# Attention and two MLPs on one Trainium2 core: sums of x on VectorE, parts of x and slices of w_out prepared over several steps, prepared weights' loads begun at the end of MLP 1

## The chip, the cores and the metric

The program runs on one NeuronCore of a Trainium2 chip. TensorE (PE) does the matrix products, VectorE (DVE), ScalarE (ACT) and GpSimd (POOL) the rest, and SyncE (SP) issues the DMAs. Every engine executes its own instructions in order and waits on semaphores for the others. The metric is the device time of one execution in microseconds (us).

## The reference

A chunked attention with eight memory keys (4 batches, 8 heads, 768 positions of 64) gives x, 3072 tokens by 512. Two MLPs follow one another, each with a hidden width of 2048:

```
h = x @ w1_in;  y = (h - tanh(h)) @ w1_out
h = y @ w2_in;  g = h if h >= 1, 0 if h <= -1, else (h + 1)^2 / 4
out = g @ w2_out
```

The weights come as 64-bit floats, all else is 32-bit. The four weight matrices of the two MLPs are rounded to 32 bits on the chip.

## The kernel before

**Precision.** Each operand of a weight product is split into a high part (rounded, by ACT: `split_to`, L203) and the rest (the low part, by VectorE, L204). A product is hi·hi + lo·hi + hi·lo. A 64-bit weight slice is rounded by two ACT passes (`round_act`, L131 and L134), three VectorE operations (L140, L141, L149) and one integer add (L153), here on GpSimd.

**MLP 1.** Tokens are cut into 6 blocks of 512, the hidden width into 16 slices of 128: 96 steps. Step s computes one hidden slice (`hidden`, 12 matmuls of 512 columns) and the output slice of step s-16 (`second`, 12 matmuls). Attention runs between the steps until about step 78. When MLP 1's steps end, 17 of its output slices are left ("old").

**Preparing MLP 2's weights.** In steps 32 to 81 the slices of w2_in are rounded, summed (`prep_sums`), split and stored to DRAM (`win`, seven tiles for each of 8 pairs). The 16 slices of w2_out go the same way to `wout` (`prep_out_*`), eight beside the w_in pairs and eight in steps 88 to 95 (`PREP_OUT`).

**MLP 2.** The first product works on pairs of token blocks (3 superblocks, `sb`) and pairs of hidden slices (8, `q`) by a scheme with seven products in place of eight on 2x2 blocks. One pair is a quad (`quad`, n = 0 to 23): the products run in the order 1, 2, 6, 5, 7, 4, 3, each 6 matmuls on a part of x (`xc`) and streamed tiles of `win` (`in`). Products 1, 6, 7, 4 accumulate in bank a; ACT copies the bank out in between as u1, u2, u3. Products 2, 5 and 3 use banks b and c, of which there is one pair. `gate2` makes the four hidden slices of a quad: an add with u1, u2 or u3 and a clamp on VectorE, a square on ACT, a maximum on VectorE. After products 2, 5, 7 and 3 stands a gap (`gap`, 0 to 3): an output slice of 12 matmuls, first the 17 old ones, then those of MLP 2, whose `ghi` (ACT) and `glo` (VectorE) are prepared one gap ahead and whose weights stream in from `wout` (`out`).

**What sets the order.** Code order is each engine's order; buffers are reused by tag, and an instruction waits until its buffer is free. Up to MLP 2 three tables of events (`before`, `rounds`, `behind`) put work at steps. SP's DMAs form one queue: x for a superblock (`x_load`, four of 512 KB), `in` (256 KB), `out` (256 KB), slices to be rounded (`stage`, 512 KB) and stores. Between superblocks x's seven parts are made in the last quad of the old superblock, each right behind the product that used the old part; the sums of x run on GpSimd (`x_sums`, L544 to L548).

Of the kernel before, what the change touches and what calls it, by code (L numbers as in the profile page):

```python
# [57 lines left out]
PREP_OUT = [37 + 7 * i for i in range(8)] + [88 + i for i in range(8)]  # L58
# [4 lines left out]
STREAM_IN, STREAM_OUT = 10, 8  # L63

# [9 lines left out]
def tile_memory_attention_two_mlps(  # L74
# [71 lines left out]
    def round_sign(phase, which, fc):  # L146
# [6 lines left out]
        nc.gpsimd.tensor_tensor(out=bits, in0=bits, in1=stage[:, :, 0], op=ALU.add)  # L153
# [38 lines left out]
    def prep_sums(q):  # L192
# [5 lines left out]
        for o, a, b in ((t1, b12, b11), (t3, b22, b12), (t2, b22, t1), (t4, b21, t2)):  # L198
            nc.gpsimd.tensor_tensor(out=o, in0=a, in1=b, op=ALU.subtract)
# [25 lines left out]
    def prep_out_load(fc):  # L225
        load_weights(1, 1, fc, "stage3" if fc < HALF else f"stage{fc % STAGES}")
# [306 lines left out]
    def x_sums(sb, part):  # L533
        f = held[sb]
        if part == 0:
            f["tags"] = []
            for i in (5, 6):
                two = [take(f"a{i}_{sb}_{k}") for k in range(2)]
                f["tags"] += [tag for tag, _ in two]
                f[i] = [t for _, t in two]  # L540
# [15 lines left out]
    def x_split(sb, i):  # L556
        if i in XWIDE:
# [7 lines left out]
        for k in range(2):  # L565
            split_to(f[:, k, :] if i not in (5, 6) else f[k], t[k], t[2 + k])
        if i == 2:
            x_sums(sb, 1)
        if i in (5, 6):
            for tag in held[sb]["tags"][2 * (i - 5):2 * (i - 4)]:  # L570
                give_later.append(tag) if i == 6 else give(tag)
        if i == 3:
            for tag in give_later:
# [86 lines left out]
    def ready(item, n, gap):  # L660
# [4 lines left out]
        return need < n - 1 or (need == n - 1 and gap >= 2)  # L665
# [143 lines left out]
    for fc in range(FC):  # L809
        p = PREP_OUT[fc]  # L810
# [11 lines left out]
    def x_give(fc):  # L822
# [156 lines left out]
```

## Time and profile before

| | us |
|---|---|
| median of 3 runs | 1178.83 |
| lowest and highest | 1177.38, 1179.82 |
| the profiled execution | 1177.54 |
| its span, first to last instruction | 1175.8 |
| PE busy | 1111.2 |
| VectorE busy | 759.8 |
| ACT busy | 556.9 |
| GpSimd busy | 155.4 |

The span is cut in 40 slices, each with the busy share in tenths. A row of the timeline says when a run of like instructions starts, how long it lasts, and in square brackets how long the engine was idle before it and who ended that. "x6" is a count; start times are us from the span's start. MLP 2 begins at about 600 us. A DMA's issue on SP is not its landing; where landing is given, it is from issue.

### The profile page before, as it was taken

To read this page: it belongs to the slowest core of one execution; us is meant where nothing else is said; L and a number is where in the kernel's file an instruction comes from. 1 tells how busy PE (TensorE), PEld (TensorE's weight loads), DVE (VectorE), ACT (ScalarE), POOL (GpSimd) and SP (SyncE) were. 2 spreads that over 40 slices of the span, in tenths; PEclk is the share of its full clock that TensorE was granted. 3 is DMA by queue.
4 is the path that set the end of the run, shared out by engine and by line. 5 is a ranking of instruction groups with operands and counts; after the bars stand their busy time and mean duration, and the time that the engine had idled before them with its cause. 6 is when DMAs were issued, how large, how long until landed. Compare 5 with 4: busy or idle time off the path is not lost.

```text
span 1175.8 us, 20216 instructions
## 1 busy us (share of the span) xinstructions
PE 1111.2 (95%) x7793; PEld 899.2 (76%) x7799; DVE 759.8 (65%) x1252; ACT 556.9 (47%) x964; POOL 155.4 (13%) x126
## 2 busy tenths in 40 slices
PE   6999999999999999999659999789999989999998
PEld 3677888888888888888448878668887868888876
DVE  4799987887887788679846554644454644353532
ACT  3566665566555566556534433423233433333321
POOL 1231220221222022025200020100020100000000
PEclk9999999999999999999969999989999999999999
DMA  9895643634644641453253465436576546556264
GB/s 232 238 264 173 165 135 99 181 113 157 198 153 127 195 155 46 153 188 126 108 196 109 151 218 195 160 115 234 188 251 224 187 148 226 183 198 233 101 227 146
DMA packets 159648, 202.67 MB, mean 172 GB/s; under 512 B 61760, under 2 KB 86336, under 8 KB 159552
## 3 DMA queue, kind: packets, MB, share of 16 engines
q1 hardware_dynamic: 159552, 201.38, 53.9%
q8 instruction: 62, 1.02, 0.4%
q14 instruction: 34, 0.28, 0.1%
HBM read 165.68 MB, written 35.65 MB: 171 GB/s over the span
## 4 chain that ended last, share of the span: by engine, by line
PE 84%; DVE 7%; ACT 4%; DMA 2%; issue 1%; SPq 1%; POOL 0%; DVEq 0%; ACTq 0%; POOLq 0%
PE h L461 21%; PE acc L496 21%; PE acc_n L496 21%; PE qa L617 10%; PE qb L617 7%; DVE xc L204 2%; PE a L365 1%; PE a L309 1%; DVE g L651 1%; ACT xc L203 1%; PE b L351 1%; DVE wlo L172 1%; DVE glo L204 1%; DMA in<-win 1%; DVE g L644 1%
## 5 line engine op out<-in xcount | busy, mean ns | idle before, releaser
L204 DVE TENSOR_TENSOR glo<-g,ghi 128x512 fp32r<-128x512 f32 x192 | 141.7, 739 | 162.2 <-ACT ghi L203 111.8
L496 PE MATMUL acc_n<-ghi,out 128*128 128x512 f32 x768 | 199.4, 398 | 18.6 <-ACT ghi L203 14.0
L496 PEld LDWEIGHTS acc_n<-ghi,out 128*128 128x128 f32 x768 | 145.6, 191 | 54.7 <-ACT ghi L203 16.0
L617 PE MATMUL qa<-xc,in 128*128 128x512 f32 x576 | 148.2, 393 | 20.2 <-DMA in<-win 20.2
L203 ACT ACTIVATE ghi<-g 128x512 fp32r<-128x512 f32 x192 | 119.5, 625 | 82.9 <-PE acc L496 48.5
L172 DVE TENSOR_TENSOR wlo<-raw,whi 128x512 fp32r<-128x512 f32 x192 | 147.9, 770 | 4.7 <-ACT whi L165 4.7
L648 ACT ACTIVATE t<-t,half 128x512 f32<-128x512 f32 x96 | 69.5, 724 | 165.2 <-DVE t L647 164.9
L153 POOL TENSOR_TENSOR raw<-raw,stage 128x512 int32<-128x512 int32 x64 | 84.2, 1316 | 461.3 <-DVE raw L149 319.0
L617 PEld LDWEIGHTS qa<-xc,in 128*128 128x128 f32 x576 | 109.1, 190 | 44.2 <-issue 20.6
L165 ACT ACTIVATE whi<-raw 128x512 fp32r<-128x512 f32 x192 | 120.5, 628 | 24.4 <-PE acc L496 17.2
L644 DVE TENSOR_TENSOR g<-qb,u 128x512 f32<-128x512 f32 x72 | 49.7, 690 | 121.9 <-ACT u L633 90.6
L633 ACT ACTIVATE u<-qa 128x512 f32<-128x512 f32 x72 | 42.9, 596 | 147.7 <-PE qa L617 147.5
L617 PE MATMUL qb<-xc,in 128*128 128x512 f32 x432 | 111.1, 393 | 1.1 <-DVE g L644 1.1
L496 PE MATMUL acc<-ghi,whi 128*128 128x512 f32 x384 | 109.6, 399 | 0.2 <-ACT y L506 0.2
L461 PE MATMUL h<-xh,whi 128*128 128x512 f32 (+2 forms) x392 | 105.7, 391 | 3.0 <-ACT whi L165 3.0
L496 PE MATMUL acc_n<-glo,out 128*128 128x512 f32 x384 | 107.0, 393 | 0.0
L496 PE MATMUL acc<-ghi,wlo 128*128 128x512 f32 x384 | 106.0, 390 | 0.2 <-DVE wlo L172 0.2
L496 PE MATMUL acc<-glo,whi 128*128 128x512 f32 x384 | 105.6, 389 | 0.0
L471 ACT ACTIVATE g<-h 128x512 f32<-128x512 f32 x96 | 57.0, 594 | 102.3 <-PE h L461 80.6
L461 PE MATMUL h<-xh,wlo 128*128 128x512 f32 (+2 forms) x392 | 104.1, 387 | 1.0 <-DVE wlo L172 1.0
L461 PE MATMUL h<-xl,whi 128*128 128x512 f32 (+2 forms) x392 | 103.8, 387 | 0.1
L617 PEld LDWEIGHTS qb<-xc,in 128*128 128x128 f32 x432 | 81.8, 190 | 19.1 <-DVE g L644 2.0
(88 smaller groups left out, 1390.0 us busy)
## 6 DMA issues: line engine op xcount, KB each, us to landing
out<-wout SPq DMA_DIRECT2D x192, 256.0 KB, 2.9
in<-win SPq DMA_DIRECT2D x168, 256.0 KB, 3.5
stage<-w_in SPq DMA_DIRECT2D x32, 512.0 KB, 5.4
stage<-w_out SPq DMA_DIRECT2D x32, 512.0 KB, 4.0
k<-qkv_t SPq DMA_DIRECT2D x80, 128.0 KB, 4.5
v<-qkv_t SPq DMA_DIRECT2D x80, 128.0 KB, 3.3
win<-preph SPq DMA_DIRECT2D x32, 256.0 KB, 3.3
yd<-y SPq DMA_DIRECT2D x24, 256.0 KB, 2.6
```

What stands on the lines that cost most here:

```text
L153: nc.gpsimd.tensor_tensor(out=bits, in0=bits, in1=stage[:, :, 0], op=ALU.add)
L165: nc.scalar.activation(out=hi, in_=r, func=AF.Copy)
L172: nc.vector.tensor_tensor(out=lo, in0=r, in1=hi.bitcast(F32), op=ALU.subtract)
L203: nc.scalar.activation(out=hi, in_=src, func=AF.Copy)
L204: nc.vector.tensor_tensor(out=lo, in0=src, in1=hi.bitcast(F32), op=ALU.subtract)
L461: nc.tensor.matmul(hp, w[:, kc * 128:(kc + 1) * 128], x[:, kc, n0:n1], start=j == 0 and kc == 0, stop=j == 2 and kc == KC - 1,)
L471: nc.scalar.activation(out=g, in_=hp, func=AF.Tanh)
L496: nc.tensor.matmul(acc_t[dm], w[:, dm * 128:(dm + 1) * 128], g, start=first and j == 0, stop=last and j == 2,)
L617: nc.tensor.matmul(bank, w[:, k * 128:(k + 1) * 128], z[k], start=first and j == 0 and k == 0, stop=j == 2 and k == 1, skip_group_check=True,)
L633: nc.scalar.activation(out=t, in_=bank, func=AF.Copy)
L644: nc.vector.tensor_tensor(out=g, in0=src, in1=plus, op=ALU.add)
L648: nc.scalar.activation(out=t, in_=t, func=AF.Square, scale=0.5, bias=half)
```

## The change

In MLP 1 the integer add of the second MLP's rounding and the sums of w_in and of x go from GpSimd to VectorE. x's first superblock is loaded at step 80 and cut in steps 82 to 91, except parts 4 and 3, which are cut in quad 0. Only eight slices of w_out are prepared in MLP 1; the others, two a quad, in quads 0 to 3 (`late_out`). The first seven `in` loads are written into steps 93 and 94. At later superblocks the sums come in quads 4, 5 and 7, parts 1 and 2 are cut in quad 6 into tiles of their own where needed (`xnext`), the others after gaps of quad 7 and of the next quad. The 17 old output slices take four gaps in quads 0 and 1 and three in quads 2 to 4 (`OLD_GAPS`), an MLP 2 slice may be used one gap earlier, and the prefetch of `out` begins in quad 3 instead of 2, `x_load` in the quad 3 of a superblock instead of its quad 4.

```diff
...
 PREP_IN, PREP_IN_EVERY = 32, 7
-PREP_OUT = [37 + 7 * i for i in range(8)] + [88 + i for i in range(8)]
+OLD_GAPS = [(0, 1, 2, 3)] * 2 + [(0, 1, 2)] * 3
...
-        nc.gpsimd.tensor_tensor(out=bits, in0=bits, in1=stage[:, :, 0], op=ALU.add)
+        eng = nc.vector if phase else nc.gpsimd
+        eng.tensor_tensor(out=bits, in0=bits, in1=stage[:, :, 0], op=ALU.add)
...
         for o, a, b in ((t1, b12, b11), (t3, b22, b12), (t2, b22, t1), (t4, b21, t2)):
-            nc.gpsimd.tensor_tensor(out=o, in0=a, in1=b, op=ALU.subtract)
+            nc.vector.tensor_tensor(out=o, in0=a, in1=b, op=ALU.subtract)
         sums_t[q] = t
...
     def prep_out_load(fc):
-        load_weights(1, 1, fc, "stage3" if fc < HALF else f"stage{fc % STAGES}")
+        load_weights(1, 1, fc, "stage3")
...
-    def x_sums(sb, part):
+    def x_sums(sb, k):
         f = held[sb]
...
+        for i in (5, 6):
+            f[i] = f.get(i, []) + [take(f"a{i}_{sb}_{k}")]
+        a11, a12, a21, a22 = (f[i][:, k, :] for i in (1, 2, 7, 4))
+        s1, s2 = f[5][k][1], f[6][k][1]
+        nc.vector.tensor_tensor(out=s1, in0=a21, in1=a22, op=ALU.add)
+        nc.vector.tensor_tensor(out=s2, in0=s1, in1=a11, op=ALU.subtract)
+        nc.vector.tensor_tensor(out=a21, in0=a11, in1=a21, op=ALU.subtract)
+    def x_sum_last(sb):
+        f = held[sb]
         for k in range(2):
-            a11, a12, a21, a22 = (f[i][:, k, :] for i in (1, 2, 7, 4))
-            if part == 0:
-                nc.gpsimd.tensor_tensor(out=f[5][k], in0=a21, in1=a22, op=ALU.add)
-                nc.gpsimd.tensor_tensor(out=f[6][k], in0=f[5][k], in1=a11, op=ALU.subtract)
-                nc.gpsimd.tensor_tensor(out=a21, in0=a11, in1=a21, op=ALU.subtract)
-            else:
-                nc.gpsimd.tensor_tensor(out=a12, in0=a12, in1=f[6][k], op=ALU.subtract)
-        if part == 1:
-            f[3] = f[2]
-    xc = {}
+            a12 = f[2][:, k, :]
+            nc.vector.tensor_tensor(out=a12, in0=a12, in1=f[6][k][1], op=ALU.subtract)
+        f[3] = f[2]
+    xc, xnext = {}, {}
...
     def x_split(sb, i):
-        if i in XWIDE:
+        if i in (1, 2) and sb % 2:
+            two = [
+                wide.tile([128, 2, N], F32R, tag=f"stage{2 * i - 2 + k}", name=f"xc{i}_{sb}_{k}") for k in range(2)
+            ]
+            t = [two[k // 2][:, k % 2, :] for k in range(4)]
+        elif i in XWIDE:
             t = xsp.tile([128, 4, N], F32R, tag=XWIDE[i], name=f"xc{i}_{sb}")
...
         for k in range(2):
-            split_to(f[:, k, :] if i not in (5, 6) else f[k], t[k], t[2 + k])
-        if i == 2:
-            x_sums(sb, 1)
+            split_to(f[k][1] if i in (5, 6) else f[:, k, :], t[k], t[2 + k])
...
-        xc[i] = t
+        xnext[i] = t
...
         need = sb * HALF + i // 2
-        return need < n - 1 or (need == n - 1 and gap >= 2)
+        return need < n - 1 or (need == n - 1 and gap >= 1)
...
         k = at[0]
+        if n < len(OLD_GAPS) and g not in OLD_GAPS[n]:
+            return flush()
         if k < len(queue) and ready(queue[k], n, g):
...
         sb, q = n // HALF, n % HALF
-        nxt = sb + 1 if q == HALF - 1 and sb + 1 < NSB else None
-        if sb + 1 < NSB:
-            if q == HALF - 4:
-                x_load(sb + 1)
-            if q == HALF - 2:
-                x_sums(sb + 1, 0)
-        if n == 2:
+        nxt = sb + 1
+        more = nxt < NSB
+        if more and q == HALF - 5:
+            x_load(nxt)
+        if n == 4:
+            spare.extend(f"prep{i}" for i in range(6))
+        if n == 3:
             for _ in range(STREAM_OUT // 2):
                 load_out([spare.pop(0) for _ in range(2)])
+        if n < 4:
+            prep_out_load(LATE_OUT[2 * n])
...
         def mult(i, bank, first):
+            if q == 0 or i not in (1, 2):
+                xc[i] = xnext[i]
             product(n, i, bank, first)
-        def done(i):
-            if nxt is not None:
+        def then(i):
+            if more and q == HALF - 1:
                 x_split(nxt, i)
+        def late_out(part):
+            if n < 4:
+                i, p = divmod(part, 2)
+                fc = LATE_OUT[2 * n + i]
+                if p == 0:
+                    if i:
+                        prep_out_store(LATE_OUT[2 * n])
+                    prep_out_act(fc)
+                    prep_out_rest(fc)
+                else:
+                    prep_out_split(fc)
+                    if i == 0:
+                        prep_out_load(LATE_OUT[2 * n + 1])
         t1, u1 = take_copy(f"u1_{n}", a)
-        done(1)
         mult(2, b, True)
         give(t1)
-        done(2)
+        if q == 0:
+            x_split(sb, 4) if sb == 0 else None
         gap(n, 0)
+        late_out(0)
+        if q == 0:
+            x_split(sb, 3)
+        if more and q == HALF - 4:
+            x_sums(nxt, 0)
+        if more and q == HALF - 2:
+            x_split(nxt, 1)
+        if more and q == HALF - 1:
+            x_sum_last(nxt)
         mult(6, a, False)
         mult(5, c, True)
-        done(5)
-        done(6)
+        then(6)
         gap(n, 1)
+        late_out(1)
+        then(5)
+        if more and q == HALF - 3:
+            x_sums(nxt, 1)
         mult(7, a, False)
         give(t3)
-        done(7)
         gap(n, 2)
+        late_out(2)
+        then(7)
+        if more and q == HALF - 2:
+            x_split(nxt, 2)
         mult(4, a, False)
         gate2(n, 1, 0, a)
-        done(4)
         mult(3, c, False)
         give(t2)
-        done(3)
         gap(n, 3)
+        late_out(3)
+        if n < 4:
+            prep_out_store(LATE_OUT[2 * n + 1])
+        then(4)
...
+    EARLY_OUT, LATE_OUT = out_fc_list(0, HALF), out_fc_list(HALF, FC)
...
             at_step(before, p + 2 + m + 0.5, prep_store, q, m)
-    for fc in range(FC):
-        p = PREP_OUT[fc]
+    for i, fc in enumerate(EARLY_OUT):
+        p = PREP_IN + 5 + PREP_IN_EVERY * i
         at_step(before, p - 2, prep_out_load, fc)
...
-    X0 = NS - 1
-    at_step(before, X0 - 9, x_load, 0)
-    at_step(before, X0 - 7, x_first)
+    def stream_in():
+        load_in(spare.pop(0))
+    X0 = NS - FC
+    at_step(before, X0, x_load, 0)
+    at_step(behind, X0 + 2, x_first)
+    at_step(behind, X0 + 3, x_sums, 0, 1)
+    at_step(behind, X0 + 6, x_sum_last, 0)
+    for i, p in ((1, X0 + 4), (2, X0 + 5), (6, X0 + 7), (5, X0 + 9), (7, X0 + 11)):
+        at_step(behind, p, x_split, 0, i)
     for fc in range(FC):
-        at_step(behind, NS - FC + fc - 1, x_give, fc)
-    for i, p in ((1, X0 - 6), (2, X0 - 5), (6, X0 - 4), (5, X0 - 3), (7, X0 - 2)):
-        at_step(behind, p, x_split, 0, i)
+        at_step(behind, X0 + fc - 1, spare.append, f"raw0_{fc}")
+    for i in range(7):
+        at_step(behind, X0 + 13 + i // 4, stream_in)
...
             output(o)
-    x_split(0, 4)
-    x_split(0, 3)
-    for i in (NS - 1, NS, NS + 1):
-        run(before, i)
-        run(rounds, i)
-        run(behind, i)
+    run(behind, NS - 1)
     spare.extend([f"{w}0_{i}" for w in ("whi", "wlo") for i in range(2)])
-    spare.extend(f"prep{i}" for i in range(6))
-    for _ in range(STREAM_IN):
-        load_in(spare.pop(0))
+    for _ in range(STREAM_IN - 7):
+        stream_in()
...
```

SP at the end of MLP 1: before, the first `in` loads (named by quad and tile) stand behind the stores of the sixteenth w_out slice.

```order
L241 DMA wout15_115<-prepoh15_7183 128x512
L241 DMA wout15_115<-prepol15_7184 128x512
L591 DMA in0_0_7189<-win0_92 128x512
L591 DMA in0_1_7191<-win0_92 128x512
L591 DMA in0_2_7193<-win0_92 128x512
```

Now they stand behind the eighth prepared slice (number 11) and ahead of the first slice that quad 0 rounds.

```order
L244 DMA wout11_111<-prepoh11_6725 128x512
L244 DMA wout11_111<-prepol11_6726 128x512
L590 DMA in0_0_7011<-win0_92 128x512
L590 DMA in0_1_7013<-win0_92 128x512
...
L590 DMA in1_1_7075<-win1_93 128x512
L590 DMA in1_2_7077<-win1_93 128x512
L121 DMA stage11_4_7079<-w2_out 128x1024
```

They have moved ahead of eight slices' loads and stores.

SP at the start of quad 3, now: `a` are the four x loads, `out` the first prefetch, `stage11_7` slice 7 of w_out.

```order
L244 DMA wout14_114<-prepol14_7670 128x512
L532 DMA a0_1_7675<-yd2_5208 128x1024
...
L532 DMA a3_1_7681<-yd3_6332 128x1024
L600 DMA out0_0_0_0_7683<-wout0_100 128x512
...
L600 DMA out0_0_3_1_7696<-wout9_109 128x512
L121 DMA stage11_7_7699<-w2_out 128x1024
L590 DMA in4_3_7717<-win4_96 128x512
```

The four x loads and the eight `out` loads, which stood apart, now stand together, between a store and the slice.

ACT in quad 3, before:

```order
L633 ACTIVATE u1_3_7749<-qa3_7741 128x512
L648 ACTIVATE t2_3_00_7763<-t2_3_00_7763,half_83 128x512
L203 ACTIVATE ghi92_7766<-g92_6960 128x512
L165 ACTIVATE whi1_92_7770<-raw01_12_2421 128x512
L633 ACTIVATE u2_3_7793<-qa3_7741 128x512
```

and now:

```order
L632 ACTIVATE u1_3_7709<-qa3_7701 128x512
L647 ACTIVATE t2_3_00_7723<-t2_3_00_7723,half_83 128x512
L206 ACTIVATE ghi91_7726<-g91_6880 128x512
L168 ACTIVATE whi1_91_7730<-raw01_11_2355 128x512
L133 ACTIVATE raw11_7_7747<-stage11_7_7699 128x512
L136 ACTIVATE stage11_7_7699<-stage11_7_7699 128x512
L632 ACTIVATE u2_3_7760<-qa3_7701 128x512
```

The two passes over the slice stand between the weights' high part and the copy u2.

## Rows read from the trace of the kernel before

**Rows 1.** Stretches: length, busy (count) PE, PEld, DVE, ACT, POOL; clock, DMA, GB/s.
```profile
665.18:685.59 20.41, 20.41 (x92) 16.89 (x91) 11.45 (x20) 8.87 (x16) 0.00 (x0) 1.00 0.30 93
...
100.00:550.00 450.00, 450.00 (x3917) 371.74 (x3916) 369.97 (x606) 274.11 (x486) 98.62 (x80) 1.00 0.47 146
...
602.00:604.00 2.00, 2.00 (x6) 1.53 (x5) 0.00 (x0) 0.40 (x1) 0.00 (x0) 0.50 1.04 394
```

**Rows 2.** The page's 40 slices: granted clock of PE in tenths.
```profile
PEclk9999999999999999999969999989999999999999
```

**Rows 3.** Busy us in the stretches with holes and one without.
```profile
558.95:611.88 52.93, 28.39 (x106) 20.70 (x104) 36.26 (x53) 23.46 (x43) 9.48 (x7) 0.81 0.39 139
694.30:755.83 61.53, 61.53 (x271) 50.71 (x272) 30.02 (x48) 22.96 (x38) 8.88 (x7) 1.00 0.63 209
755.83:799.54 43.71, 33.24 (x121) 25.13 (x119) 23.97 (x37) 15.66 (x28) 2.35 (x2) 0.84 0.33 109
880.00:884.40 4.40, 1.63 (x8) 1.01 (x7) 3.09 (x5) 1.84 (x4) 0.00 (x0) 1.00 0.00 0
941.00:974.30 33.30, 28.10 (x114) 21.82 (x113) 16.90 (x29) 11.42 (x20) 0.00 (x0) 0.95 0.41 141
```

**Rows 4.** Timeline of PE at the first edge: start, length, what, idle before.
```profile
600.67 2.90 PE L617 MATMUL qa<-xc,in 128*128 128x512 f32 x6 [20.19 <-DMA in<-win]
```

**Rows 5.** Timeline of SP's queue at the first edge.
```profile
597.57 8.90 SPq L591 DMA_DIRECT2D in<-win  x12
```

**Rows 6.** Timeline of PE at the second edge.
```profile
755.83 1.52 PE L617 MATMUL qa<-xc,in 128*128 128x512 f32 x6
763.96 3.78 PE L496 MATMUL acc_n<-ghi,out 128*128 128x512 f32 x8 [6.61 <-ACT ghi L203]
...
770.98 1.52 PE L617 MATMUL qb<-xc,in 128*128 128x512 f32 x6
```

**Rows 7.** Timeline of ACT at the second edge.
```profile
755.86 2.19 ACT L203 ACTIVATE xc<-a 128x512 fp32r<-128x512 f32 x4 [0.59 <-PE qb L617]
...
763.29 1.13 ACT L203 ACTIVATE ghi<-g 128x512 fp32r<-128x512 f32 x2
```

**Rows 8.** Timeline of PE at two block ends.
```profile
884.34 2.24 PE L496 MATMUL acc_n<-ghi,out 128*128 128x512 f32 x8 [2.77 <-ACT yn L506]
...
974.24 2.25 PE L496 MATMUL acc_n<-ghi,out 128*128 128x512 f32 x8 [0.24 <-ACT yn L506]
```

**Rows 9.** Timeline of VectorE ahead of the first of these.
```profile
875.38 1.77 DVE L651 TENSOR_TENSOR g<-g,t 128x512 f32<-128x512 f32 x1
```

**Rows 10.** Timeline of VectorE in an undisturbed quad.
```profile
678.25 0.69 DVE L644 TENSOR_TENSOR g<-qb,u 128x512 f32<-128x512 f32 x1 [3.63 <-ACT u L633]
678.98 0.43 DVE L647 TENSOR_SCALAR t<-g 128x512 f32<-128x512 f32 x1
```

**Rows 11.** Timeline of GpSimd ahead of the block end at 884.
```profile
874.88 1.73 POOL L544 TENSOR_TENSOR a<-a,a 128x512 f32<-128x512 f32 x1
```

**Rows 12.** Instructions on w_out's slices, 480 to 600 us: ns min/median/max; landing in us.
```profile
L131 ACT ACTIVATE raw<-stage x12: 656/660/665, 488.1 to 592.0; 128x512 f32<-128x512 f32 x12
...
L149 DVE SCALAR_TENSOR_TENSOR raw<-stage,raw x12: 691/693/694, 489.7 to 593.6; 128x512 int32<-128x512 int32 x12
L153 POOL TENSOR_TENSOR raw<-raw,stage x12: 1277/1308/1830, 490.7 to 594.5; 128x512 int32<-128x512 int32 x12
...
DMA to landing us min/median/max: 3.5/4.0/7.4
```

**Rows 13.** The four x loads of 680 to 700 us, the same view.
```profile
L529 SPq DMA_DIRECT2D a<-yd x4: 423/428/1867, 683.4 to 686.3; - x4
...
DMA to landing us min/median/max: 5.6/6.9/8.1
```

**Rows 14.** The eight loads of w_out slices of 640 to 660 us.
```profile
L601 SPq DMA_DIRECT2D out<-wout x8: 320/384/636, 642.7 to 646.5; - x8
...
DMA to landing us min/median/max: 4.4/6.0/6.3
```

More of the change, by code (lines that the diff above doesn't have):

```diff
@@ L531, in x_load @@
         held[sb] = {1: y[0], 2: y[1], 7: y[2], 4: y[3]}
-    def x_sums(sb, part):
+    def x_sums(sb, k):
         f = held[sb]
-        if part == 0:
[L536 to L540, printed above, removed]
-        for k in range(2):
-            a11, a12, a21, a22 = (f[i][:, k, :] for i in (1, 2, 7, 4))
-            if part == 0:
-                nc.gpsimd.tensor_tensor(out=f[5][k], in0=a21, in1=a22, op=ALU.add)
-                nc.gpsimd.tensor_tensor(out=f[6][k], in0=f[5][k], in1=a11, op=ALU.subtract)
-                nc.gpsimd.tensor_tensor(out=a21, in0=a11, in1=a21, op=ALU.subtract)
-            else:
-                nc.gpsimd.tensor_tensor(out=a12, in0=a12, in1=f[6][k], op=ALU.subtract)
-        if part == 1:
-            f[3] = f[2]
-    xc = {}
+        for i in (5, 6):
[7 more added lines that the diff above has]
+        f = held[sb]
+        for k in range(2):
+            a12 = f[2][:, k, :]
+            nc.vector.tensor_tensor(out=a12, in0=a12, in1=f[6][k][1], op=ALU.subtract)
+        f[3] = f[2]
+    xc, xnext = {}, {}
     XWIDE = {1: "xh0", 2: "xl0", 4: "xh1", 3: "xl1"}
@@ L565, in x_split @@
         for k in range(2):
-            split_to(f[:, k, :] if i not in (5, 6) else f[k], t[k], t[2 + k])
-        if i == 2:
-            x_sums(sb, 1)
+            split_to(f[k][1] if i in (5, 6) else f[:, k, :], t[k], t[2 + k])
         if i in (5, 6):
[L570 to L573, printed above, removed]
+            for tag, _ in f:
                 give(tag)
-            give_later.clear()
-        xc[i] = t
-    give_later = []
+        xnext[i] = t
     in_order = [(n, m) for n in range(NSB * HALF) for m in range(7)]
@@ L764, in quad, with out_fc_list @@
         give(t2)
-        done(3)
         gap(n, 3)
+        late_out(3)
+        if n < 4:
+            prep_out_store(LATE_OUT[2 * n + 1])
+        then(4)
+    def out_fc_list(a, b):
+        return [out_fc(i) for i in range(a, b)]
+    EARLY_OUT, LATE_OUT = out_fc_list(0, HALF), out_fc_list(HALF, FC)
     before, rounds, behind = {}, {}, {}
@@ L820, in x_first @@
         x_sums(0, 0)
-    def x_give(fc):
-        spare.append(f"raw0_{fc}")
-    X0 = NS - 1
-    at_step(before, X0 - 9, x_load, 0)
-    at_step(before, X0 - 7, x_first)
+    def stream_in():
[7 more added lines that the diff above has]
+        at_step(behind, p, x_split, 0, i)
     for fc in range(FC):
-        at_step(behind, NS - FC + fc - 1, x_give, fc)
-    for i, p in ((1, X0 - 6), (2, X0 - 5), (6, X0 - 4), (5, X0 - 3), (7, X0 - 2)):
-        at_step(behind, p, x_split, 0, i)
+        at_step(behind, X0 + fc - 1, spare.append, f"raw0_{fc}")
+    for i in range(7):
+        at_step(behind, X0 + 13 + i // 4, stream_in)
     def warm(n, ps):
```

## The prediction

> **What bounds the kernel now.** I read the busy share by slices first, then stretches of the second half, then PE, SP, ACT and VectorE in order of time at each hole, last the DMA landings.
>
> PE is the bound. From 100 to 550 us it is busy for all of 450.00 us [rows 1]; it idles or slows in three later places, where the slices of PE's clock dip [rows 2]. Free of waits, PE does one 512-column matmul every 61.53 / 271 = 0.227 us [rows 3], so a product (6 matmuls) takes 1.36 us and an output slice (12) 2.72. What a stretch takes beyond that is lost:
> - end of MLP 1 and first edge, 558.95 to 611.88: 52.93 - 106 x 0.227 = 28.9
> - second edge, 755.83 to 799.54: 43.71 - 121 x 0.227 = 16.2
> - 880.00 to 884.40: 4.40 - 8 x 0.227 = 2.6
> - third edge, 941.00 to 974.30: 33.30 - 114 x 0.227 = 7.4
>
> Together 55.1 us [rows 3].
>
> At the first edge PE stops at 600.67 - 20.19 = 580.5 and starts again at 600.67, when the first prepared part of w_in lands; its first 6 matmuls take 2.90 us [rows 4] at a granted clock of 0.50, 1.2 of 2.4 GHz [rows 1]; SP issues that load at 597.57, behind the stores of the last slice of w_out [rows 5]. At the second edge PE waits from 757.2 to 763.96 for a gate's high part, ghi [rows 6]. ACT wrote that at 763.29, behind the parts of x it had to cut [rows 7]. At 884 the wait is for block-end copies on ACT [rows 8]; a few us earlier VectorE's operations stretch from 0.69 to 1.77 us [rows 9, 10] while GpSimd adds sums of x [rows 11].
>
> **The change part by part.** *Early loads.* Seven loads of prepared w_in stand on SP right behind the last store of a w_out slice in MLP 1, now around step 88 of 96. They need only tiles freed by step 91, so they land before quad 0. The second half of w_out's slices leaves steps 88 to 95, and with it the chain over ACT, VectorE, GpSimd and DMA that makes the first of the waits; x's parts are cut over steps 84 to 91. So I count the 28.9 as gone. What is late next is quad 0's own work, below.
>
> *Second and third edge.* One part of x is now cut after each gap, and x1 and x2 already in quad 6 into other tiles. In quad 7 VectorE gets 10 more operations of at most 0.69 us [rows 10] beside 20 in 11.45 us of a 20.41-us quad [rows 1], and each ghi stands on ACT behind at most two cuts of 0.55 us [rows 7]. 16.2 and 7.4 go. With the sums off GpSimd the 2.6 goes. A wait for the copies at each block end stays, about 0.4 us with PE's refill, read off the 0.24 at 974.24 [rows 8]: three times, 1.2. Removed: 55.1 - 1.2 = **53.9**.
>
> *Sums and the integer add on VectorE.* Between 100 and 550 us VectorE has 450.0 - 370.0 = 80 us free [rows 1]. Added there are 24 integer adds and 32 half-width sums (at most 0.69 each, 22 us). The add on VectorE is in no row. Its nearest neighbours are the other integer operation at 0.69 and the same add on GpSimd at 1.31 [rows 12]; I take 0.7, the nearest by engine, with 0.43 (a one-input operation [rows 10]) and 1.31 as ends. Even at 1.31 it is 31 + 22 = 53 us of 80, so it hides behind PE and costs 0. The cover is gone at (80 - 22) / 24 = 2.4 us an add. GpSimd's stretching of VectorE goes too; PE hides that gain.
>
> The Trainium skill (GPSIMD Engine Reference, 4.1 Engine selection) says that GpSimd adds 32-bit integers exactly and natively while the ordinary elementwise path computes in fp32, so VectorE needs another way, whose price no run here shows. [...]
>
> *Quads 0 to 3: the new work.* Each prepares two slices of w_out: ten VectorE operations (about 0.43 + 0.43 + 0.69 + 0.7 + 0.69 = 2.9 us a slice), so 11.5 + 5.9 = 17.4 of 20.4 us; in quads 2 and 3, whose fourth gap is now empty, about 16.2 of 17.7. VectorE and ACT serve gates, slices and splits in order, so I followed both queues by hand with 0.57 us per VectorE operation (11.45 / 20) and 0.55 per ACT pass (8.87 / 16) [rows 1], and 4.0 us from a slice's load to its landing [rows 12]:
> - quad 0: x4 is cut ahead of gap 0 and the last block's four copies stand behind it. They end at 10.3 us after the quad's start; PE wants their banks at 8.2 for gap 1: 2.3 with refill.
> - quads 1 and 2: the first slice's load stands on SP behind the stores of the slice before. ACT waits for it with the copy of u2 behind; product 7 must not start before u2 is read: 1.0 and 1.1. Gap 0 waits for its late whi: 0.5 and 0.7.
> - quad 3's product 2 needs quad 2's bank pair, whose last reader on VectorE stands behind slice 14's rounding; with the fourth gap empty only product 1 covers it: 2.4.
>
> Together **8.0**; ends 0 and, if VectorE turns out the bound, 16.
>
> *The pile-up in quad 3.* Ahead of slice 7's load, SP now issues four x loads of 512 KB and eight of w_out of 256 KB: with the slice 4.7 MB, all in one queue. Before, the eight stood in quad 2 and the four in quad 4, and nothing on ACT waited behind them. Let T be the end of quad 2's last product. The stores before these loads wait for slice 14's low part, by my queues at about T + 7, so the loads start at T + 7.3. PE is ready for product 7 at T + 4 x 1.36 + 2 x 2.72 + 2.4 = T + 13.3. How long 4.7 MB take no row shows. Alone, the four took 683.4 to 686.3 + 8.1, so 11.0 us, the eight 642.7 to 646.5 + 6.3, so 10.1, and a slice 4.0 [rows 12, 13, 14]: 25 one after the other is the upper end. At the best rate shown, 394 GB/s [rows 1], 12.0 is the lower. I take 15 (about 315 GB/s), nearer the low end, since on one queue they overlap. Then ACT makes two passes of 0.66 and copies u2, 1.9 in all. PE's wait: 7.3 + 15 + 1.9 - 13.3 = **10.9**; ends 7.9 and 20.9. After 6.8 us of idle PE needed 770.98 - 763.96 = 7.0 us for 18 matmuls worth 4.1 [rows 6]; I add that **2.9** for the slow clock.
>
> The Trainium skill (DMA: Bandwidth & Descriptors, Queues, rings and completion order) says that each DMA engine takes a ring's descriptors in order, though completions need not be. By it the slice, issued last, lands about last, which speaks against rival A; no run here shows these three kinds in one burst.
>
> **Sum.** 8.0 + 10.9 + 2.9 - 53.9 = -32.1. The profiled execution took 1177.54 us (span 1175.8), 1.3 under the median of the runs shown: 1177.5 - 32.1 = 1145.4; I say **1145.5**.
>
> **Rivals.** *A. The pile-up is hidden.* Then 10.9 + 2.9 stay saved: 1131.7. For it: the kernel before moved the same 4.2 MB with no wait of PE. Against: there no ACT instruction ahead of u2 waited for the queue's last load. Chance 0.17.
>
> *B. Quads 0 to 3 are bound by VectorE and ACT, or the loads come one by one.* Small waits 16 and a pile-up of about 16 with its clock: 16 + 16 + 2.9 - 53.9 = -19.0, so 1158.5. For it: 16.2 of 17.7 us of VectorE with waits in between. Against: 0.43 us for the add would loosen it. Chance 0.14.
>
> *C. The first edge's wait stays,* as the early loads are held by a tile or a store: some 20 us come back, 1165. Against: their tiles are freed by step 91. Chance 0.04.
>
> *D. Slower: the add on VectorE breaks MLP 1.* Beyond 2.4 us an add, VectorE has more than PE's time in the preparing steps and wlo and glo come late; each further us costs 24. The kernel is slower than before from 2.4 + 32.1 / 24 = 3.7 us an add; at 4.5 it takes 1145.4 + 24 x 2.1 = 1195.8. For it: the operation is in no row. Against: three of VectorE's kinds over this tile stay under 0.7 us. Chance 0.04.
>
> **How the numbers follow.** Forecast 0.61, A 0.17, B 0.14, C 0.04, D 0.04. The forecast's own range is 1138 to 1153, from the ends of the pile-up and about 4 us of small waits. With A below and most of B above, 8 in 10 lie in 1127 to 1160; the floor with nothing new late is 1177.5 - 53.9 = 1123.6. A change of 0.2% (2.4 us) is about what a measurement of this kernel can tell. Every case but D is well past that: faster 0.95, same 0.01, slower 0.04.
>
> **What the profile after would show.** Right: PE goes from MLP 1 into quad 0 without a hole; the first load of prepared w_in is issued tens of us before quad 0; no wait over 1 us in quads 6 to 8 and 14 to 16; one hole of 8 to 14 us in quad 3, ended by ACT's u2, itself behind the first ACT pass of a w_out slice, and slow matmuls behind it; VectorE's 0.69-us operations no longer stretched after the first weights are done. Wrong: no hole in quad 3 (A); waits of 2 us and more in every gap of quads 0 to 3 (B); PE waiting on wlo or glo between 270 and 550 us (D).

## The result and the profile after

The changed kernel takes 1145.88 us (median of 4 runs, 1144.44 to 1147.70); the kernel before takes 1178.82. The ratio is 0.9722, with an interval from 0.9705 to 0.9740. The profiled execution took 1147.70 us with a span of 1145.9, 29.8 less than the profiled execution of before.

The granted clock of PE in the page's 40 slices, to set beside [rows 2]: one dip is left of two.

```profile
PEclk9999999999999999999999989999999999999999
```

PE's waits from MLP 2's start to the end, by who ended them (total us, times, longest). The wait for an `in` load [rows 4] and the waits for ghi [rows 6] are gone; the block ends wait 1.6 in five places. New are u2 and whi, in quads 1 to 3; the waits for the last block's copies y and for a gate's g have grown.

```profile
PE qa L616 <- ACT u L632: 9.7, 3, 8.5
PE qb L616 <- DVE g L643: 3.7, 3, 2.2
PE acc_n L499 <- ACT yn L509: 1.6, 5, 0.6
PE acc L499 <- ACT y L509: 1.5, 1, 1.5
PE acc L499 <- ACT whi L168: 1.0, 2, 0.5
```

Stretches of the changed kernel, columns as in [rows 1]: quads 0 to 4, then the burst of loads in quad 3.

```profile
576.85:600.11 23.26, 21.43 (x91) 16.58 (x90) 15.90 (x28) 12.30 (x22) 0.00 (x0) 1.00 0.54 169
600.11:623.03 22.92, 21.33 (x91) 16.62 (x90) 16.81 (x30) 12.03 (x21) 0.00 (x0) 1.00 0.56 173
623.03:642.45 19.42, 18.67 (x79) 14.33 (x78) 14.28 (x25) 12.03 (x21) 0.00 (x0) 1.00 0.52 168
642.45:674.94 32.49, 21.75 (x79) 17.01 (x78) 16.66 (x30) 11.08 (x19) 0.00 (x0) 0.79 0.72 250
674.94:694.25 19.31, 18.02 (x79) 14.56 (x78) 14.08 (x25) 7.85 (x14) 0.00 (x0) 1.00 0.37 119
649.11:664.30 15.19, 8.53 (x37) 6.67 (x35) 3.02 (x5) 1.77 (x3) 0.00 (x0) 0.84 1.02 363
```

Quads 0 and 1 need 20.41 us, the others, with their fourth gap empty, 17.69. They lose 2.85, 2.51, 1.73, 14.80 and 1.62: 23.5 us of the gain given back, most of it in quad 3. There PE shows two holes:

```profile
642.45 1.52 PE L616 MATMUL qa<-xc,in 128*128 128x512 f32 x6
646.22 2.93 PE L616 MATMUL qb<-xc,in 128*128 128x512 f32 x6 [2.24 <-DVE g L643]
...
652.04 1.52 PE L616 MATMUL qa<-xc,in 128*128 128x512 f32 x6
...
666.13 2.93 PE L616 MATMUL qa<-xc,in 128*128 128x512 f32 x6 [8.50 <-ACT u L632]
```

SP's queue of the changed kernel: ten `in` loads from 538.80, where before the first was issued at 597.57 [rows 5]; in quad 3 the four x loads, the eight `out` loads and, last, slice 7.

```profile
538.80 22.68 SPq L590 DMA_DIRECT2D in<-win  x10
...
649.11 1.94 SPq L532 DMA_DIRECT2D a<-yd  x4
651.09 6.85 SPq L600 DMA_DIRECT2D out<-wout  x8
658.30 0.33 SPq L121 DMA_DIRECT2D stage<-w_out  x1
```

ACT behind it: it waits 12.18 us for the slice, passes over it twice, and only then copies u2, for which product 7 waits.

```profile
664.38 0.66 ACT L133 ACTIVATE raw<-stage 128x512 f32<-128x512 f32 x1 [12.18 <-DMA stage<-w_out]
664.94 0.67 ACT L136 ACTIVATE stage<-stage 128x512 int32<-128x512 uint32 x1
665.50 0.58 ACT L632 ACTIVATE u<-qa 128x512 f32<-128x512 f32 x1
```

The integer add on VectorE, which no row of before showed (ns, shortest, median, longest): one instruction on 16-bit halves, 0.69 us.

```profile
L156 DVE CUSTOM_DVE_ANT_0 raw<-stage,raw x32: 693/693/695, 209.2 to 675.8; 128x1024 uint16<-128x1024 uint16 x32
```

### The profile page after: what moved, and what is told of

The parts are those of the page before. It is cut to its first block, busy times and chain, and to the rows that moved or that the text cites. A ratio compares the mean times of both kernels' runs of the same rounds, so it can differ in the third digit from the quotient of the medians.

```text
span 1145.9 us, 20140 instructions
## 1 busy us (share of the span) xinstructions
PE 1107.9 (97%) x7799; PEld 897.1 (78%) x7799; DVE 759.2 (66%) x1340; ACT 556.0 (49%) x964; POOL 42.6 (4%) x38
## 3 DMA queue, kind: packets, MB, share of 16 engines
q8 instruction: 62, 1.02, 0.4%
## 4 chain that ended last, share of the span: by engine, by line
PE 84%; DVE 7%; DMA 4%; ACT 3%; SPq 1%; issue 1%; DVEq 0%; ACTq 0%
PE h L464 23%; PE acc_n L499 22%; PE acc L499 19%; PE qa L616 9%; PE qb L616 7%; PE a L368 1%; DMA start<-qkv_t 1%; PE a L312 1%; DMA in<-win 1%; DVE g L650 1%; PE b L354 1%; DMA stage<-w_out 1%; DVE g L643 1%; DVE t L646 1%; DVE glo L207 1%
## 5 line engine op out<-in xcount | busy, mean ns | idle before, releaser
L207 DVE TENSOR_TENSOR glo<-g,ghi 128x512 fp32r<-128x512 f32 x192 | 132.6, 690 | 156.7 <-ACT ghi L206 105.7
L499 PE MATMUL acc_n<-ghi,out 128*128 128x512 f32 x768 | 194.2, 391 | 1.6 <-ACT yn L509 1.6
L499 PEld LDWEIGHTS acc_n<-ghi,out 128*128 128x128 f32 x768 | 143.3, 188 | 34.8 <-ACT yn L509 5.4
L175 DVE TENSOR_TENSOR wlo<-raw,whi 128x512 fp32r<-128x512 f32 x192 | 134.7, 702 | 4.7 <-ACT whi L168 4.7
L616 PEld LDWEIGHTS qa<-xc,in 128*128 128x128 f32 x576 | 108.6, 189 | 33.9 <-ACT u L632 11.5
L475 DVE TENSOR_TENSOR g<-h,g 128x512 f32<-128x512 f32 x96 | 66.1, 688 | 47.8 <-ACT g L474 47.6
```

The source lines that it names most:

```text
L175: nc.vector.tensor_tensor(out=lo, in0=r, in1=hi.bitcast(F32), op=ALU.subtract)
L207: nc.vector.tensor_tensor(out=lo, in0=src, in1=hi.bitcast(F32), op=ALU.subtract)
L475: nc.vector.tensor_tensor(out=g, in0=hp, in1=g, op=ALU.subtract)
L499: nc.tensor.matmul(acc_t[dm], w[:, dm * 128:(dm + 1) * 128], g, start=first and j == 0, stop=last and j == 2,)
L616: nc.tensor.matmul(bank, w[:, k * 128:(k + 1) * 128], z[k], start=first and j == 0 and k == 0, stop=j == 2 and k == 1, skip_group_check=True,)
```

## The experiments

| run | what | us | ratio to before, interval |
|---|---|---|---|
| changed | | 1145.88 | 0.9722 (0.9705 to 0.9740) |
| e1 | slice 7's load ahead of the burst | 1143.81 | 0.9696 (0.9680 to 0.9713) |
| f2 | burst behind slice 15's load | 1134.65 | 0.9628 (0.9613 to 0.9642) |
| e2 | four old slices in quads 0 to 3 | 1149.50 | 0.9744 (0.9729 to 0.9758) |
| e5 | cuts of x at the block edge | 1148.58 | 0.9738 (0.9721 to 0.9755) |
| f3 | before, with the queue's rules alone | 1162.55 | 0.9867 (0.9850 to 0.9883) |
| e4 | adds and sums on GpSimd | 1146.28 | 0.9727 (0.9710 to 0.9744) |
| e3 | all slices in MLP 1 | 1133.77 | 0.9611 (0.9595 to 0.9627) |
| f1 | e3 with two sets of buffers | 1128.73 | 0.9576 (0.9562 to 0.9590) |
| g1 | f1, one step earlier | 1126.10 | 0.9553 (0.9540 to 0.9566) |
| h1 | before, two sets of buffers | 1172.76 | 0.9949 (0.9935 to 0.9963) |
| h3 | h1, `in` loads written earlier | 1163.76 | 0.9871 (0.9853 to 0.9888) |

**The pile-up (e1, f2).** e1 moves two lines:

```diff
+        if n < 4:
+            prep_out_load(LATE_OUT[2 * n])
         if more and q == HALF - 5:
             x_load(nxt)
...
-        if n < 4:
-            prep_out_load(LATE_OUT[2 * n])
```

> In quad 3 the load of w_out's slice 7 is written ahead of the four x loads and the eight out loads; nothing else changes. In the changed kernel SP issued the x loads at 649.11 us, the slice at 658.30, and it landed at 664.3; PE stood for 8.5 us before product 7 and then needed 6.1 us for work worth 4.1. Theory (ACT's pass over the slice, with u2 behind it, waits for a load that stands at the end of a burst on SP): the slice is issued at about 649, lands by 655, ACT is through at 657, and PE wants product 7 at 657.5. Hole and slow matmuls go: 8.65 + 2.0 = 10.7 us less than the changed kernel's 1145.9, so 1135 us. Rival 1 (the twelve other loads take the DMA engines from the slice, wherever it stands): it still lands after 660, the hole stays at 4 us or more, 1140 or above. Rival 2 (the x and out loads or the in loads behind them become late in turn): the hole in quad 3 goes, but PE waits for a DMA in quad 4 or 5.

Product 7 no longer waits, but the time is hardly less. PE and ACT of e1 show where the hole went: ACT now waits for slice 15's load, which stands behind the same burst, and PE waits 8.70 us before product 2 of quad 4. That is rival 2, with a slice as the late load.

```profile
670.07 2.93 PE L616 MATMUL qb<-xc,in 128*128 128x512 f32 x6 [8.70 <-DVE g L643]
```

```profile
665.68 0.66 ACT L133 ACTIVATE raw<-stage 128x512 f32<-128x512 f32 x1 [7.42 <-DMA stage<-w_out]
```

So f2 puts the burst (the x and `out` loads) behind both slices of the quad:

```diff
         late_out(2)
+        if n == 3:
+            x_load(nxt)
+            for _ in range(STREAM_OUT // 2):
+                load_out([spare.pop(0) for _ in range(2)])
         then(7)
```

> The four x loads and the eight out loads of quad 3 stand behind the load and the rounding of the quad's second slice (15), just ahead of product 4, instead of ahead of its first slice. With the first slice alone moved ahead, the hole moved: slice 15 was issued at 659.67, landed about 6 us later, and PE waited 8.7 us before product 2 of quad 4 for VectorE, which stood behind that slice. Theory (any slice behind the burst on SP holds ACT and VectorE, and they hold PE): both holes go, and nothing of a slice is behind the burst any more; 8.65 + 2.0 less than the changed kernel: 1135 us. The wait before product 2 of quad 3 (2.2) stays. Rival (the burst costs PE its time wherever it stands: now the sums of x in quad 4 wait for the x loads, with the gates behind them on VectorE): a hole of 5 us or more in quad 4, 1140 us or above.

It took 1134.65, as the theory said. The burst itself is no shorter: its last load, issued at 667.6, takes 5.5 us or more to land, 16 us after the first issue at 657.12. But PE is busy for 15.09 of the row's 17.08 us, where it was for 8.53 of 15.19:

```profile
657.12:674.20 17.08, 15.09 (x67) 12.14 (x66) 13.92 (x25) 8.87 (x15) 0.00 (x0) 1.00 1.00 356
```

**The second and third edge (e2, e5, f3).** e2 changes one line, e5 puts the cuts back:

```diff
-OLD_GAPS = [(0, 1, 2, 3)] * 2 + [(0, 1, 2)] * 3
+OLD_GAPS = [(0, 1, 2, 3)] * 4
```

> The old output slices take all four gaps in quads 0 to 3 and the first of quad 4, instead of four in quads 0 and 1 and three in quads 2 to 4. Theory (with the fourth gap empty, only product 1 covers VectorE's queue ahead of product 2): the waits before product 2 in quads 3 and 4 of the changed kernel, 2.4 and 1.3 us with 1.7 and 0.3 of slow matmuls behind them, 5.8 in all, go; but the loads of quad 3 start no earlier after quad 2's start (26.1 us) while PE reaches product 7 some 2.4 us sooner after it, so the hole there grows from 8.65 to about 11.1. Net 3.3 us less: 1142.5 us. Rival (the waits before product 2 come from the slices' work on VectorE and stay whatever stands in the fourth gap): they stay at 2.4 and 1.3 us, and the time stays at 1146 or more.

```diff
-        if more and q == HALF - 2:
-            x_split(nxt, 1)
...
         t1, u1 = take_copy(f"u1_{n}", a)
+        then(1)
         mult(2, b, True)
...
+        then(2)
```

> For the second and third superblock the parts of x are cut in the last quad again, each right behind the product that used the old part, and the last sum behind part 2, as in the kernel before; the sums stay on VectorE and in quads 4, 5 and 7. Theory (ghi stands on ACT behind cuts that wait for PE to finish with the old part): PE waits for ghi again in quads 7 and 15, and most of 16.2 + 7.4 us comes back; with 1.2 that stay anyway, about 20 more than 1145.9: 1166 us, with 14 or so at the second edge and 6 at the third. Rival (the holes came from the sums on GpSimd, which stretched VectorE's operations from 0.69 to 1.77 us): with the sums on VectorE less than 6 us comes back, under 1152.

Both theories failed. In e5 PE waits for ghi only 2.2 us in two places, one at each edge, and its interval overlaps the changed kernel's; its rival, the sums on GpSimd, would fit that time, but see f3. In e2 the waits before product 2 in quads 3 and 4 went and the hole in quad 3 was 11.5 us, as expected; but PE waits in quads 4, 7 and 8 came up, of which two are these:

```profile
751.82 2.14 PE L499 MATMUL acc_n<-ghi,out 128*128 128x512 f32 x8 [0.88 <-ACT ghi L206]
...
769.47 2.12 PE L499 MATMUL acc_n<-ghi,out 128*128 128x512 f32 x8 [1.25 <-ACT ghi L206]
```

That sent me back to PE of the kernel before. From the start of quad 8 (775.06) five products follow one another with no output slice (`acc_n`) between them:

```profile
775.06 1.52 PE L617 MATMUL qa<-xc,in 128*128 128x512 f32 x6
776.42 1.52 PE L617 MATMUL qb<-xc,in 128*128 128x512 f32 x6
777.88 1.67 PE L617 MATMUL qa<-xc,in 128*128 128x512 f32 x6
780.00 1.67 PE L617 MATMUL qb<-xc,in 128*128 128x512 f32 x6 [0.46 <-DVE g L644]
781.70 1.67 PE L617 MATMUL qa<-xc,in 128*128 128x512 f32 x6
786.52 3.32 PE L496 MATMUL acc_n<-ghi,out 128*128 128x512 f32 x8 [3.14 <-ACT ghi L203]
```

Gap 1 of quad 7 is empty in the same way (755.83 follows product 5 at once, [rows 6]). No slice was ready. The slice of the next gap then had its high part made in that gap itself instead of one gap ahead. At the third edge no gap is empty, but ACT of before shows the same late preparation, and no cut near it: it was idle for 4.84 us ahead of u3 and then wrote two ghi at once, while PE waited 3.15 us.

```profile
958.14 0.60 ACT L633 ACTIVATE u<-qa 128x512 f32<-128x512 f32 x1 [4.84 <-PE qa L617]
959.96 0.72 ACT L648 ACTIVATE t<-t,half 128x512 f32<-128x512 f32 x1 [1.22 <-DVE t L647]
960.59 1.13 ACT L203 ACTIVATE ghi<-g 128x512 fp32r<-128x512 f32 x2
```

```profile
961.25 3.63 PE L496 MATMUL acc_n<-ghi,out 128*128 128x512 f32 x8 [3.15 <-ACT ghi L203]
```

Three gaps stay empty in either kernel. Before, they fell into quads 7 and 8; the change puts them at the ends of quads 2, 3 and 4, and lets a slice be used one gap sooner. f3 takes only these two rules over into the kernel before:

```diff
+        if n < len(OLD_GAPS) and g not in OLD_GAPS[n]:
+            return flush()
...
-        return need < n - 1 or (need == n - 1 and gap >= 2)
+        return need < n - 1 or (need == n - 1 and gap >= 1)
```

> The kernel before, with two things alone taken from the change: the old output slices take four gaps in quads 0 and 1 and three in quads 2 to 4, and a slice of MLP 2 may be used one gap earlier (from gap 1). Sums, cuts, weights and loads are as before. The trace of before shows gaps left empty for want of a ready slice: gap 1 of quad 7, gaps 0 and 1 of quad 8; and the slice of the next gap had its high part made in that gap itself. Theory (the second and third edge cost PE time because the queue of output slices had run dry, so that no slice was ready a gap ahead; the cuts alone do not): most of 16.2 + 7.4 us goes, some 3 stay; 1178.8 - 20 = 1159 us, and the first edge is as before. Rival (the cuts at the block edge and the sums on GpSimd cost it, as the prediction put it): the two edges stay within 5 us of what they were, 1174 us or above.

It gains 16.3 us (1178.87 to 1162.55), near the theory and far from the rival. Its waits, with the cuts and GpSimd's sums where they were:

```profile
PE qa L618 <- DMA in<-win: 20.8, 1, 20.8
PE acc_n L497 <- ACT yn L507: 4.1, 5, 2.8
PE qb L618 <- DVE g L645: 3.6, 3, 2.3
PE acc_n L497 <- ACT ghi L204: 2.2, 2, 1.1
```

The wait for ghi fell from 14.0 us in four places to 2.2; the block-end wait of 2.8 [rows 8] and the first edge are untouched. The sums are on GpSimd here, so e5's rival does not hold. The 2.2 us that f3 and e5 have left are two waits of 1.1 for a ghi right behind a cut: what the cuts still cost with the new rules.

What f3 does not tell is which of its two rules counts, and e2 shows that the empty gaps by themselves cost little. e2's queue runs dry too: six products in a row around the start of quad 8 (761.51), and the slices of gap 1 in quads 7 and 8 have their high part made in that gap. Yet its waits for ghi are 2.1 us, and 121 matmuls there take 31.53 us, 4.1 lost, where as many took 43.71 before [rows 3].

```profile
758.79 1.52 PE L616 MATMUL qa<-xc,in 128*128 128x512 f32 x6
760.15 1.52 PE L616 MATMUL qb<-xc,in 128*128 128x512 f32 x6
761.51 1.52 PE L616 MATMUL qa<-xc,in 128*128 128x512 f32 x6
...
766.69 1.52 PE L616 MATMUL qb<-xc,in 128*128 128x512 f32 x6
```

```profile
748.05:779.58 31.53, 28.31 (x121) 22.10 (x120) 20.24 (x35) 14.84 (x27) 0.00 (x0) 1.00 0.45 142
```

e2 hands out the gaps as the kernel before does, but has the sooner use and the spread cuts. In the kernel before a late ghi falls into gap 2, where ACT makes it behind product 7's u3 and the gate's square (958.14 to 960.59 above); in e2 it falls into gap 1, where no such gate stands between the copy and the ghi (u2 at 768.32, ghi at 768.80). That speaks for the sooner use as the rule that counts. It stands in f3, e2 and e5 alike and was not run alone, nor were the spread cuts with the old rules, so this part stays open.

**The moves to VectorE (e4).**

```diff
-        eng = nc.vector if phase else nc.gpsimd
+        eng = nc.gpsimd
```

and the same for both kinds of sums.

> The changed kernel with its VectorE moves undone: the integer add (1.31 us on GpSimd, 0.69 on VectorE in the changed kernel's trace), the sums of w_in and the sums of x are on GpSimd again; all else as changed. Theory (in MLP 1 PE hides them; in quads 0 to 3 the add stands in the chain of each slice, ahead of ACT's high part and the copies behind it): about 1 us for some four of the eight slices, none elsewhere, as the sums of x now fall into quads without a block end: 1146 + 4 = 1150 us, from 1147 to 1154. Rival 1 (the moves carry much of the gain, by GpSimd stretching VectorE's operations to 1.77 us): 1158 us or above. Rival 2 (they are worth nothing): within 1 us of 1146.

Rival 2 holds: 1146.28 against 1145.88, as a balance: the wait for u2 in quad 3 grew to 10.4 us and waits for wlo came to 2.6, while others shrank. In the slices of quads 0 to 3 the add takes 1.43 us on GpSimd:

```profile
L156 POOL TENSOR_TENSOR raw<-raw,stage 128x512 int32<-128x512 int32 x8 | 11.4, 1431 | 126.8 <-DVE raw L151 126.8
```

The waits at block ends stay at 1.6 us in five places, though the sums of x are on GpSimd again. So the 2.6 us at 884 did not go by the change of engine. That the sums left the quad ahead of a block end is the likely reason; it was not tried alone.

**The first edge (e3, f1, g1, h1, h3).** e3 prepares all sixteen slices in MLP 1:

```diff
-    for i, fc in enumerate(EARLY_OUT):
-        p = PREP_IN + 5 + PREP_IN_EVERY * i
+    for i, fc in enumerate(EARLY_OUT + LATE_OUT):
+        p = PREP_IN + 5 + PREP_IN_EVERY * i if i < HALF else 80 + i
```

> All sixteen slices of w_out are prepared in MLP 1 again, the second eight in steps 88 to 95 with four stage buffers as in the kernel before; all else is as in the changed kernel (integer add and sums on VectorE, x cut over steps 84 to 91, in loads written into steps 93 and 94). Quads 0 to 3 lose their slices' work. The question is what took the 28.9 us at the first edge. Theory (the slices were tied to one another: each takes one raw buffer and one pair of parts, so the next begins when the last is cut; 6.8 to 7.5 us a slice before, with the add at 1.3 on GpSimd, some 6.2 now, against 5.44 us a step; and the in loads stood behind the last store): now four in loads stand ahead of the last three stores, so PE loses only about 8 x 0.8 = 6 us at the end of MLP 1, and the 23.9 us that the changed kernel loses in quads 0 to 4 mostly go: 1145.9 - 23.9 + 7 = 1129 us. Rival (the slices in these steps cost what they cost before, wherever the other parts stand): 28.9 come back, 1145.9 - 23.9 + 28.9 = 1151 us.

1133.77 is near the theory: the slices may stand in steps 88 to 95. What is left is a wait in quad 0, for a u1 that stands on ACT behind the last slices.

```profile
586.78 2.93 PE L616 MATMUL qa<-xc,in 128*128 128x512 f32 x6 [4.95 <-ACT u L632]
```

f1 adds a second set of buffers:

```diff
-        round_act(1, 1, fc, tag="prep0")
+        odd = fc in LATE_OUT and LATE_OUT.index(fc) % 2
+        round_act(1, 1, fc, tag="prep1" if odd else "prep0")
```

and a second pair of tiles for the high and low parts in the same way.

> As the run with all sixteen slices in MLP 1 (1133.8 us), but the second eight alternate between two raw buffers and two pairs of parts. In that run ACT's first pass of a slice waited 2.4 to 2.6 us in each of steps 90 to 95 for VectorE's low part of the slice before, slices ended 9 us after MLP 1, and in quad 0 the copy u1 stood behind them: PE waited 4.95 us before product 6, and quad 0 lasted 30.1 us where 20.4 are needed. Theory (the single set of buffers ties the slices together): the waits on ACT go, the last slice ends within 2 us of MLP 1, and quad 0 loses 2 us instead of 9.7: 1133.8 - 7.7 = 1126 us. Rival (VectorE's work in these steps, 5.3 to 6.5 us for a step of 5.44, is the bound): the slices end as late as before, and the time stays within 2 us of 1133.8.

5 of the 7.7 us came. The row of f1's last steps shows PE busy throughout and VectorE for 35.07 of 37.30 us: it has little time left there, as the rival said, though the rival's time did not come.

```profile
543.20:580.50 37.30, 37.30 (x166) 30.70 (x165) 35.07 (x62) 26.19 (x46) 0.00 (x0) 1.00 0.61 208
```

g1 starts the second eight slices one step earlier (79 + i for 80 + i) and cuts x4 behind gap 0.

> As the run with all slices in MLP 1 and two sets of buffers (1128.7 us), with the second eight slices begun one step earlier (87 to 94) and x's part 4 cut behind gap 0 of quad 0 instead of ahead of it. In that run VectorE worked without a pause from 543 to 580 us, the last slice ended 5.6 us after MLP 1, and ACT's copies of the last block (y) ended 3.9 us after PE wanted their banks for gap 1; with the slow matmuls behind it quad 0 lasted 26.4 us instead of 20.4. Theory (quad 0 is late by VectorE's queue: the slices' tail and the cut of x4 ahead of the copies): one step earlier takes the tail away (about 4 us), the cut 1.2 more; the wait falls to 0.5 or less and the slow matmuls with it: 1128.7 - 5 = 1124 us. Rival (VectorE is full from step 84 on, so an earlier start moves nothing, and only the cut's 1.2 us comes): 1127 us.

1126.10, between the two and nearer to the rival. The wait for y falls from 3.9 to 1.7 us. g1 beats both kernels, at a ratio of 0.9553 (0.9540 to 0.9566).

h1 gives the kernel before two sets of buffers, and nothing else:

> The kernel before, with one thing changed: the second eight slices of w_out, in steps 88 to 95, alternate between two raw buffers and two pairs of parts. In loads still stand behind the last store, the integer add is on GpSimd, nothing is moved to MLP 2. Theory (the first edge's 28.9 us came from slices tied to one another by the one buffer, 6.8 to 7.6 us each, so that the last store was issued 17 us after MLP 1's end): slices now take about 5.4 to 6 us, the last store is issued some 5 us after MLP 1, the first in loads land 3 us later; the waits of PE in MLP 1 (3 to 4 us) shrink too. 1178.9 - 14 = 1165 us. Rival (the order on SP, with the loads behind the stores, or the add on GpSimd cost it): within 4 us of 1178.9.

Only 6 us came, and the theory's size was wrong. ACT's waits from 545 to 600 us say why. Before:

```profile
ACT raw L131 <- DVE prepol L204: 18.7, 7, 4.8
ACT prepoh L203 <- POOL raw L153: 3.0, 2, 2.6
```

In h1 (545 to 595) the first row is gone and the second has grown: the add on GpSimd was the next tie.

```profile
ACT prepoh L203 <- POOL raw L153: 11.6, 7, 4.2
```

h3 writes the first seven `in` loads of h1 into steps 93 and 94 as well.

> The kernel before with two sets of buffers for the second eight slices (1172.8 us), and besides the first seven in loads written into steps 93 and 94, ahead of the stores of the last three or four slices, as the change writes them. With the two sets alone MLP 1 ended at 577.55 us and the last store and the first in load were still issued at 591.77 and 592.14; PE waited 18.1 us. Theory (two chains end late there, the loads behind the stores and ACT's queue behind the slices' tail): the loads now land by 577, PE does products 1 and 2 and gap 0 at once, and then waits for the copy u1, which stands on ACT behind the last slice's high part at 590.4; it goes on at 591.6 with 5.4 us of work done, where it started at 595.7 with none. 1172.8 - 9.5 = 1163 us, and a wait of some 8.6 us before product 6 of quad 0. Rival 1 (the loads' place was the whole of it): 1172.8 - 18 - 3 of slow matmuls = 1152 us. Rival 2 (nothing of the kind): within 3 us of 1172.8.

It took 1163.76, and PE of h3 shows the wait where the theory put it, now on u1:

```profile
591.52 2.93 PE L619 MATMUL qa<-xc,in 128*128 128x512 f32 x6 [7.98 <-ACT u L635]
```

## Why the prediction came out right, and where its reasons did not

**The pile-up in quad 3 (right).** Predicted 10.9 and measured 8.65 (666.13 less the 657.48 at which PE was free), by the same terms. The loads began 6.7 us after quad 2's end (7.3 predicted), the 4.7 MB took 15.3 (15), ACT 1.75 (1.9). PE came to product 7 at 15.0 instead of 13.3, since the matmuls behind product 2 were slow: 5.82 us (646.22 to 652.04) for work of 4.08, granted 0.71 on the average. With those behind the hole (6.09 for 4.08) the slow clock took 3.75 us; I had counted 2.9, for one of the two places. f2 shows that this is the cause: with the burst elsewhere 11.2 us go, and no wait over 2.3 us is left in quads 3 and 4.

The burst's 4.7 MB in 15.3 us are 309 GB/s; with the other loads and stores beside them the core moved 363 in that stretch at a DMA share of 1.02, f2's 356. The Trainium skill (DMA: Bandwidth & Descriptors, Specifications) gives about 358 GB/s as one core's limit at HBM and 435 as the ceiling of the fabric. The trace does not bear out the first as a limit here: over ten microseconds of the burst the core moved 398. It stays under the second.

```profile
655.00:665.00 10.00, 2.64 (x12) 1.86 (x10) 0.00 (x0) 0.62 (x2) 0.00 (x0) 0.74 1.04 398
```

f2 moved the burst without shortening it. Whether another order would shorten it was not tried.

**The small waits (near in sum, one place missed).** 8.0 predicted. Measured in quads 0 to 2 and at product 2 of quad 3: 2.85 + 2.51 + 1.73 + 2.41 = 9.5. The 2.4 at product 2 of quad 3 came to the tenth. Quad 4 loses 1.62 more in the same way, since the fourth gap of quad 3 is empty too, which makes 11.1; I had not followed the queue that far.

**Removed (sum right).** 29.8 saved and 23.5 given back make 53.3; 53.9 was predicted. Of the parts:

- *First edge, 28.9: gone, and for the reason given, but it is not the only cure.* The prediction said that the slices' chain leaves steps 88 to 95. h1 and h3 show several ties there, each hiding the next: the single set of buffers, the add on GpSimd, the loads behind the stores, u1 behind the tail. f1 leaves the slices where they were and undoes the ties, and gains more than moving the slices, since quads 1 to 4 then lose next to nothing.
- *Second and third edge, 16.2 and 7.4: gone, but the reason given was not the one that counts.* The step "each ghi stands on ACT behind at most two cuts" named the cuts. With the cuts put back (e5) 2.2 us of waits for ghi return; with the cuts left alone and the queue's rules changed (f3) 16.3 us go. No slice was ready a gap ahead, so ghi was made late. I read who wrote it [rows 7], and not why it had not been asked for a gap earlier. Which of the two rules cures this stays open, as said under f3.
- *884, 2.6: gone, and the change of engine was not the reason* (e4).

**The integer add (right).** 0.7 taken, 0.693 measured, and hidden in MLP 1: VectorE was busy 373 of the 450 us from 100 to 550, PE all of them but 0.4. The Trainium skill (GPSIMD Engine Reference, 4.1 Engine selection) sets GpSimd's exact integer add against an ordinary path in fp32; here the row of L156 shows that VectorE does the add by a single special instruction on 16-bit halves.

**Rivals and range.** A, B, C and D did not come about. The stated upper end of 1153 does not follow from its own terms: the pile-up's upper end of 20.9 alone gives 1145.4 + 10.0 = 1155.4. The time agreed to 0.4 us of the median and 2.2 of the profiled execution; part of that is luck, as a pile-up 2.2 us too long made up for waits that were missed, and as 23.6 us of the gain came in full though the reason given for them was not the one that counts.

## What to carry to other kernels

Where a queue feeds gaps in an order written by hand, count for each gap whether an item is ready, before reading which instruction was late: an empty gap shows as products with nothing between them. The empty gap need not be the cost (e2); ask also what the late item then stands behind on its engine. Keep a load on which an in-order engine will wait out of the way of prefetches on the same queue; moving the one load ahead only hands the wait to the next. Where several ties end at one place, undoing one gives back little, and the next must be named before the price is set.

## What was not expected of the hardware

A wait of PE as short as 2.24 us (646.22) was followed by 6 matmuls in 2.93 us, at a granted clock of 0.50, against 1.52 without a wait, in the changed kernel. At the same place a wait as long was followed by 1.66 us in e1, at a granted clock of 1.00, and by 1.67 in f2:

```profile
643.39 1.66 PE L616 MATMUL qb<-xc,in 128*128 128x512 f32 x6 [2.23 <-DVE g L643]
```

```profile
644.60 1.67 PE L616 MATMUL qb<-xc,in 128*128 128x512 f32 x6 [2.24 <-DVE g L643]
```

What tells the slow case from the others was not tried.
